# A fifth query normaliser broadcast through DRAM: block 1 of the second linear-attention layer goes from matmul to DMA

## The chip, the cores and the metric

The kernel runs on one core of a Trainium2 chip. The metric is the device time of one execution in microseconds (us), as the median of several runs. The profile is of one more execution; its *span* is 1.7 us shorter than its time (327.5 against 329.18 us before). Engines are named as in the profile: PE (TensorE matmul), PEld (its weight loads), DVE (VectorE), ACT (ScalarE), POOL (GpSimd), SP (SyncE, which issues the DMAs here).

## The reference, cut to what matters

Four layers A, B, A, B on x of 2048 rows by 512 channels, 32 heads of 16 channels, each with a LayerNorm ahead of it and a residual addition behind it. The change lies in the second layer A, a linear attention whose queries pass through two softmaxes:

```python
pq = einsum(q, w_phi)
phi_q = concat([softmax(pq), softmax(-pq)])       # phi_k likewise
kv = einsum("bhsf,bhsd->bhfd", phi_k, v);  z = phi_k.sum(over s)
num = einsum("bhqf,bhfd->bhqd", phi_q, kv)
den = einsum("bhqf,bhf->bhq", phi_q, z) + 1e-6
o = num / den                                     # then @ wo, + x
```

The kernel keeps the plain exponentials `Eq` and multiplies them by one factor per head, sign and position, `rho` = 1/(softmax sum x den). That is the **query normaliser**. `rho` has one row per head, `Eq` has 16 rows per head, so `rho` has to be broadcast 16-fold over partitions.

## The kernel before

The 2048 rows are cut into four blocks of 512. Each stage of a block is a set of small steps; `_ORDER`, a list made beforehand, says in which order all steps of the program are issued, `_CHOICE` says which of the copies and residual additions go to DVE or ACT, and `_SLOTS` which buffer each tile gets. The stage of the query normaliser for layer `L`, block `b`:

```python
_OPT = {"rho_dma": ((0, 2), (0, 3), (1, 2), (1, 3)), ...}   # (layer, block): broadcast by DMA

def s_a3(self, L, b, dma):
    def md(): ...      # PE: 32 matmuls, Eq x z -> denominators in PSUM
    def dr(): ...      # DVE: times 1/softmax sum, both signs added -> Ds
    def ln(): ...      # ACT: Ds -> 1/Ds, as exp(-ln)
    def rho(): ...     # DVE: rS * Ds -> rho, 128 x 2 x 128, bf16

    # by matmul
    def bc(s):         # PE: 16 matmuls with a 0/1 matrix repeat the rows into 4 PSUM tiles
        T["pb", s] = pb = [self.ps() for _ in range(4)]
        for hb in range(NB):
            for t in range(4):
                nc.tensor.matmul(pb[t][:, hb * P:(hb + 1) * P], lhsT=self.indB[32 * t:32 * t + 32, hb, :, :],
                                 rhs=T["rho"][32 * t:32 * t + 32, s, :], start=True, stop=True, tile_position=(32 * t, 0))
    def mulp(s, t, direct):    # DVE: Eq *= PSUM tile (or its SBUF copy by ACT, made by bev)
        ev = self.Eq[L, b][s][:, t, :, :]
        src = T["pb", s][t] if direct else T["bs", s, t]
        nc.vector.tensor_tensor(out=ev, in0=src[:].rearrange("p (a i) -> p a i", a=NB), in1=ev, op=ALU.mult)

    # by DMA; pitch = 16 * 128
    def wr():          # SP: rho to DRAM, 64 KB
        self.RD[L, b] = rd = self.dram.tile([8, 2, pitch], BF16, name="rd%d%d" % (L, b))
        a = rd[0:1, 0, 0:P]
        dst = bass.AP(a.tensor, a.offset, [[P, 16], [2 * pitch, 8], [pitch, 2], [1, P]])
        nc.sync.dma_start(out=dst, in_=T["rho"][:])
    def rdb(s):        # SP: read back, each row to 16 partitions, 512 KB
        rd = self.RD[L, b]
        T["P", s] = pr = self.med([4, NB, P], "Prho")
        a = rd[0:1, s, 0:P]
        src = bass.AP(a.tensor, a.offset, [[2 * pitch, 8], [0, 16], [1, 16 * P]])
        nc.sync.dma_start(out=pr[:].rearrange("p t a i -> p (t a i)"), in_=src)
    def muld(s):       # DVE: one multiplication for half a block
        ev = self.Eq[L, b][s]
        nc.vector.tensor_tensor(out=ev[:], in0=ev[:], in1=T["P", s][:], op=ALU.mult)
    ...                # md, dr, ln, rho; then wr, rdb(0), rdb(1), muld(0), muld(1)
                       # or, for s in 0, 1: bc(s), then 4 times bev(s, t) and mulp(s, t)
```

Behind this stage, block by block: the product `mo` (PE, `Eq` x kv), its eviction `ev` to `oT`, four output matmul groups `mm`, the residual additions `res`, and the LayerNorm of the next layer. (Cuts are marked by "..." or by a comment in place of a body.)

Of the kernel before, what the change touches and what calls it, by code (L numbers as in the profile page):

```python
# [16 lines left out]
P = 128  # L17
NJ = 16
D = 512
H = 32  # L20
# [18 lines left out]
    "rho_dma": ((0, 2), (0, 3), (1, 2), (1, 3)),  # L39
    "tr_dma": (('B0', 1), ('B0', 2), ('B0', 3), ('A1', 0), ('A1', 1), ('A1', 2), ('B1', 1), ('B1', 2), ('B1', 3)),  # L40
    "fold_dma": (),
    "half_k": ((0, 3), (1, 3)),
    "half_ln": (),
    "split": ((1, 2), (1, 3)),
    "v_dram": (),
    "half_mo": (),
    "rho_pad": 0,
# [10 lines left out]
av 8 i i i i i i i i i i i i 0 f 0 g e 2t 0 bs 9 h a d c 0 j k t i i j l 27 o p 3 3 d6 b 1x 1x t 1y o m 2 2 1q  # L58
1z 1x 1x q u t r 1q v x w n s 1r w 1s 4 20 y 21 1x 22 1x 23 1q 1q 1q 1q 1v 1w z 3d 3d 3d 1u 1t 25 3e 3e 3e z 5
3e 3e z z 26 10 18 18 d5 1 z 16 11 4i 15 6 1h 13 3d 3e 3e 25 25 26 18 25 18 12 26 26 28 26 26 26 26 19 12 28  # L60
2a 28 1h 18 14 12 12 1a 28 1c 3e 2g 2g 1f 2h 2h 1h 1h 1b 1i 2b 1b 1e 1d 29 2j 2k 1h 1j 1n 2r 1b 1l 2s 1b 2c 2r
1k 2s 17 2g 2g 2h 2h 1k 1k 2h 2h 2h 2h 2d 1g 2d 2d 2d 2e 2j 1m 35 36 32 2o 2o 33 2s 33 32 33 33 2r 2s 2s 1o 2o
2o 2d 2r 3a 1k 3a 1p 2p 2o 24 24 2s 24 2u 2v 35 37 2u 2u 2u 2s 2i 2w 2j 3a 2s 3a 2l 2z 2j 24 32 32 34 2m 3b 33
3d 3f 3f 2z 2z 2z 33 2f 33 33 2f 2f 2f 3a 3a 2q 2q 2q 30 3a 2n 3a 3a 2z 3e 2q 2x 35 35 b6 3b 3a 2y 31 31 31 31
3c 3c 38 3c 39 3c 3m 3f 3n 3o 3o 3o 24 24 3g 3g 3g 3f 3p 3q 3g 3g 3g 3g 3g 3r 3q 3f 3g 24 3h 3i 3i 5l 5m 5n 3p
3s 3q 3j 3k 3k 3t 3q 3p 3x 5m 3w 3u 3h 3i 3i 3q 3v 3q 3q 3y 3h 3i 3q 3i 3h 3i 3q 5l 5o 5p 5r 5m 5q 7 7 3z 3q
3i 3j 3k 5m 5l 5s 3k 7 7 5m 5m 5m 3h 3i 7g 40 5u 44 41 42 5t 5m 5m 3j 3j 7h 7i 3k 5v 5m 5w 43 7h 45 7j 45 60
3k 3k 3k 46 45 45 5y 5x 5z 61 61 48 47 47 61 49 47 4a 47 4b 62 47 4b 63 3j 4g 94 4c 45 4d 45 4e 4f 3k 45 45 61
64 63 4h 4p 65 95 7j 7j 66 4q 63 96 95 97 97 63 67 7h 63 67 69 7h 6b 4k 4k 4k 4l 4p 4r 4k 4m 4p 4p 4s 4t 7k 7n
6a 68 6c 4o 7m 50 50 4u 4u 4u 4n 4u 7l 4w 97 7o 7p 7p 7q 7s 3l 4x 7r 7r 7p 7t 7p 6o 7u 50 7r 7r 7v 6o 6j 4v 4y  # L70
4j 6o 6q 6o 4j 4z 6k 6p 6r 6j 7r 6e 6l 95 6d 95 7v 6t 6s 6f 6d 7w 6e 7z 7x 98 9b 9a 99 6g 7y 9c 6e 6j 6j 9d 9d
6u 9d 6e 6n 80 6m 9d 6h 6v 6v 9e 9h 9f 6i 9g 9f 6w 6v 6v 6w 6w 9f 9i 9f 87 88 8h 9j 9f 50 82 9j 9l 6w 6x 6x 87
87 6w 81 83 9n 6x 9k 87 8b 89 51 51 51 51 52 52 8c 8c 8e 6u 6u 6u 9m 8j 8a 8d 8c 6v 6y 3l 8f 82 9o 82 85 82 50
51 52 4z 4z 4z 9q 9q 9s 8c 6z 8g 6y 6z 9r 71 70 6y 6y 6z 6z 72 86 a0 a0 a1 73 84 8i 74 75 74 74 50 74 8i 76 8i
77 a2 76 79 53 53 54 55 54 a5 56 53 54 9v 78 76 9q 9q 76 a0 81 53 9v 9w 9p 7a 57 9v 9u a7 76 7a 9t 8j 7c 9y 54
58 59 59 59 9v 59 9x 7d 7e 5a 8j 8j 7b 7f 5c 5b 5d 5b 5b a0 8k 5e 5b 5f 8k 9z a7 5b 5f 5j 8k 8k 8l a3 5i b4 a4
b7 5h b4 b4 b4 8l 5g b5 b5 a7 b5 b5 a7 8k 8l 8j c3 8i c3 b8 c4 c4 c4 c4 a8 8m a8 a8 a8 c3 a9 a9 5k at c1 b5 a6
8m au au c1 c2 b5 c2 aw c2 c2 a8 a9 b5 b5 8n 8o 8n 8p 8m at au at at 8n 8q 8m a7 aa 8n aw 8r 8s au au au 8s 8s
8t au au 8s 8v a6 a6 8u aa 8w aa 8x 8u 8u 8u 8y ab ac ab ad a6 aa b7 8u b9 b7 c3 8y 90 92 c1 91 c1 c2 8z c2 c2
aw ay ab c2 ba ae ab af aw b0 c4 c4 b1 bc ag ag ag ag ah bc aj ak bc c1 c4 c4 bc al ax c3 ai ai ai bd b1 ai am  # L80
93 bf bi bg az bf ai am ar bf bf bg bg aq b7 bg bg bg bg bg bb an ao ag ag ap bi ag ag b1 b1 bc b2 c2 bi bn bi
bl bk as bq br br bq br br bq bq b1 br by by by by bt b3 b3 b3 b3 br be be be br br bz c5 c5 bh bj bn bn bn c5
bu c4 by by by by c6 bo by c6 c6 c5 bt bt bt bn bv c6 c6 c6 bz be bp bp bw bm bp bp c0 c0 by c6 c6 bx c0 c0 c9
c5 ca c6 cb cb cc cb cd ce cd fr fs c7 c8 c7 c8 c8 ft cc ci cf cd cg cd c7 c8 c8 fs fu c8 e2 fu ch cd e3 cd cc
cj ck e4 cd c7 c8 c8 c7 e3 e2 cm cd c8 e6 e7 fu cl cd cd cn cp co e5 e3 hb e3 cr e2 ea e9 cq hc cs e3 cs e8 e3
e3 hd eb ec e3 e3 e3 ed ct cv hc eh cs he ee cs ef cw eg ei cx ei ei cu ei cu cu cu fs cy fs fv ej cu cy d0 cz
ek d2 fw fx fz d3 cs cs fy cs cs g0 g0 g0 el ek em ek en ek d4 d1 dc g1 eo ek g2 g3 g2 dc de eo es g0 g4 dd dh
g2 g5 g2 he hc eq g6 d7 d8 d7 d7 d7 he di dc g2 dc d9 ep er hc et dn hf da db df dh dh dh hi hh hj hg hk hk hk
dj dk dl dm dm g6 g7 g9 dn dn dg ga f0 f0 hl hm hn hm ho hm ev ew f1 hk dn g8 do do hp f2 fa fc hm hq do do dp
ev ex fc gb ev f0 dp ey dn f3 f0 hm fc f4 hq ev ez fc do dp dn dq dq d6 f5 f6 dm dm eu hs gi gj gi fd gs hr fd  # L90
ht fd hu hv fd dq fe fe f5 f5 f8 f5 f9 f7 fb gk fd fe fc gn gn gp gi gi gl gm gd gd gd ge ic gf i7 i7 i9 gg i8
dr dr dt ds dr du hx hy gd dq gu dr dv gn gq gh i7 ff ia gu fb go ff fg fh fb fb eu gv gc gn i2 gr i3 hx hz hx
i7 i2 ib gv i4 hx i1 gc hw i2 i2 i5 gu i0 gu gv gv gw gt ie fg fi if i6 ie id gw if dw dx id gv gw id id ie ie
if if ig dw ff ig if ig fg fj dw e0 dw ff fg fk ie fl fm fl fn gu fl fl fp ih ih ih ih e1 ii ii ii ik ij fq dy
gt gt gt fo fo il io io io io ii im ip iq ip is ir ir ih ii in ip ip iu it ir gx ir gy gx gx gx gz gy h0 dz dz
iv gy h1 h4 gx gy h2 h4 iw iv h5 h5 h6 h7 gy h4 h3 h5 h8 h9 h7 h7 h4 h5 ha h7
# [4 lines left out]
    "0011111111111001110111111010000010010000000000000001011111101100100000110101000110000010000001110111"  # L101
    "1101011110010000110101000000000000001101011000000000100100000000000000000101111100000011011000000000"
    "0000000000001101111010000000100101011111010000011001110111000000000000000111111011101110010100101000"
    "00000000000001111001000000000000000000000000000000000000000000000000000000000001111"
# [5 lines left out]
        "0123456701231231456204632073205712053720457604356704213560421356720415763215063506432506"  # L110
    ),
    "med": (
        "0123456789abcdef5837ae98eeaeae471853bc9e43cbe47199ce3185413cebf94c8f74e3581bc71931bc7f370bf9ac21584e"
        "af9c37214a0b589dec37"
    ),
    "t2": (
        "0123450123450342150132451032451032451032451302153421530421503452014520345123045130425123504321504321"
        "5043215043210451023134"
    ),
    "ps": (  # L120
        "0123456701234750613250746132074365462150743510635127035164051362731405263710452763210743562107423251"
        "0764376215043762435107625407152367423167052341760543210675432170652147053624036542076314257603415203"
        "6415026734107534105234065265346053460562036207346201542015471204712603712035764120356471032516407324"
        "6735012463754021637261350247613025476130746513072463501742635017463015276301562703152760432764327014"
        "6570324650324705613245076"
# [4 lines left out]
class _Fast:  # L130
# [162 lines left out]
    def setup(self):  # L293
        nc, const = self.nc, self.const
        nc.scalar.preload_act_table_set("natural_log_exp_and_others")
        self.WA = const.tile([P, NB, 3 * D], BF16, name="WA")
        self.WoA = const.tile([P, NB, D], BF16, name="WoA")
        self.WB = const.tile([P, NB, 3 * D], BF16, name="WB")
        self.WoB = const.tile([P, NB, D], BF16, name="WoB")
        self.phis = const.tile([P, NB, DH], BF16, name="phis")  # L300
        self.x = [const.tile([P, 4, D], BF16, name="x%d" % b) for b in range(4)]
        with nc.allow_non_contiguous_dma(reason="tiny w_phi load"):
            nc.scalar.dma_start(out=self.phis[:], in_=self.A_w_phi.rearrange("(hb hl) d f -> (hl d) hb f", hb=NB))
        self.wraw = {}
        self.RD = {}
        self.VD = {}
        self.constants()
# [275 lines left out]
    def s_a1(self, L, b):  # L583
# [96 lines left out]
        m = 2 if (L, b) in _OPT["half_k"] else 4  # L680
        for t in range(0, 4, m):
# [89 lines left out]
    def s_a3(self, L, b, dma):  # L771
# [46 lines left out]
        pitch = (16 + _OPT["rho_pad"]) * P  # L818
# [100 lines left out]
    def s_b1(self, L, b):  # L919
# [51 lines left out]
        def vwr():  # L971
            self.VD[L, b] = self.dram.tile([P, NB * KVW], BF16, name="vd%d%d" % (L, b))
            nc.sync.dma_start(out=self.VD[L, b][:], in_=T["V"][:].rearrange("p c t -> p (c t)"))

        def vrep(dl):
# [4 lines left out]
            if (L, b) in _OPT["v_dram"]:  # L980
                a = self.VD[L, b][dl:dl + 1, 2:3]
                src = bass.AP(a.tensor, a.offset, [[2, 4], [4 * NB * KVW, H], [1, VGW]])
# [835 lines left out]
```

## Time and profile before

| | before |
|---|---|
| time, median of 3 runs | 328.98 us (328.91 to 330.25) |
| span of the profiled run | 327.5 us |
| busy: PE, DVE, ACT | 310.3, 302.2, 279.3 us |
| DVE idle in the span | 327.5 - 302.2 = 25.3 us |

The chain of waits of the kernel before (start, duration, what; consecutive instructions of an engine are one line) is followed back only to 219.08 us. From there to 223.7 us it is mostly DVE's multiplications:

```profile
219.08 0.60 DVE Eq L816
...
220.62 3.08 DVE Eq L816 x6
...
223.74 0.57 PE ps L900 x16
```

L816 is `mulp`. This is block 1, the block of the change. SP's timeline shows block 2, which goes by DMA already: its write, and its two reads.

```profile
214.45 0.62 SPq L824 DMA_DIRECT2D rd<-rho  x1
216.66 1.38 SPq L831 DMA_DIRECT2D Prho<-rd  x2
```

Block 1's eight multiplications lie at 218.4 to 223.7 us.

### The profile page before, as it was taken

Reading aid. Unit: us, or ns where it says so; the run is one execution under the profiler, and the core shown is the slowest. Engines: PE = TensorE matmul, PEld = TensorE weight load, DVE = VectorE, ACT = ScalarE, POOL = GpSimd, SP = SyncE. Lnnn points to the kernel's source line nnn. Section 1 sums busy time; section 2 is a strip of 40 time slices with the busy share of each in tenths; the row PEclk is TensorE's granted clock in tenths of the full one; section 3 lists DMA queues with packets and bytes.
Section 4 is the critical chain, followed back from the end, with each engine's and each line's share of the span. In section 5 each row is a group of like instructions: output and inputs, shape, how many; then the busy total and the mean of one; then the engine's idle time right before and its main releaser. Section 6 shows DMA issues by size and latency. Waiting matters only on the chain. (4 is left out here: it accounts for less than half of the span.)

```text
span 327.5 us, 8033 instructions
## 1 busy us (share of the span) xinstructions
PE 310.3 (95%) x3176; PEld 149.5 (46%) x3203; DVE 302.2 (92%) x439; ACT 279.3 (85%) x634; POOL 25.3 (8%) x50
## 2 busy tenths in 40 slices
PE   7999999999999999999999999979999999999873
PEld 3655456445444444443444455644544454433221
DVE  7998995998998999899999999699999999999993
ACT  5999988998888999989999999798999996676550
POOL 4000000000021003000000000000000208400000
PEclk9999999999999999999999999999999999999999
DMA  7980000004556899998750300023436977679952
GB/s 197 380 197 3 0 2 4 2 20 120 105 148 135 152 164 133 139 121 154 137 135 1 67 3 2 4 59 90 128 58 125 179 146 134 150 139 158 166 176 92
DMA packets 37388, 35.41 MB, mean 108 GB/s; under 512 B 23008, under 2 KB 32224, under 8 KB 37344
## 3 DMA queue, kind: packets, MB, share of 16 engines
q1 hardware_dynamic: 36816, 34.81, 53.6%
q8 instruction: 27, 0.44, 0.6%
q14 instruction: 17, 0.14, 0.2%
q10 hardware_dynamic: 528, 0.02, 0.1%
HBM read 10.50 MB, written 2.36 MB: 39 GB/s over the span
## 5 line engine op out<-in xcount | busy, mean ns | idle before, releaser
L927 PE MATMUL ps<-xnT,WB 128*128 128x512 bf16 x384 | 87.6, 380 | 0.5 <-DMA xnT<-xn 0.5
L1081 DVE TENSOR_TENSOR pav<-PT,Vg 128x4096 bf16<-128x4096 bf16 (+1 forms) x34 | 72.0, 2162 | 1.5 <-DMA Vg<-V 1.0
L1019 DVE TENSOR_TENSOR prod<-QT,K 128x4096 bf16<-128x4096 bf16 x32 | 72.5, 2291 | 0.3 <-ACT QT L192 0.2
L927 PEld LDWEIGHTS <-WB 128*128 128x128 bf16 x384 | 42.3, 114 | 43.3 <-issue 5.8
L520 PEld LDWEIGHTS <-oT 128*128 128x128 bf16 x256 | 23.8, 97 | 34.5 <-ACT oT L192 5.7
L192 ACT CAST oT<-ps 128x512 bf16<-128x512 f32 (+1 forms) x60 | 32.1, 587 | 8.4 <-PE ps L1090 7.1
L706 ACT ACTIVATE Eq<-ps 128x512 bf16<-128x512 f32 x64 | 34.0, 615 | 0.7 <-PE ps L698 0.6
L520 PE MATMUL ps<-WoB,oT 128*128 128x512 bf16 x122 | 32.1, 380 | 2.4 <-ACT oT L192 2.0
L599 ACT ACTIVATE Ek<-ps 128x512 bf16<-128x512 f32 x64 | 33.6, 622 | 0.4 <-PE ps L593 0.2
L698 PE MATMUL ps<-xnT,WA 128*128 128x512 bf16 x128 | 30.7, 380 | 0.6 <-DVE Eq L816 0.6
L540 ACT ACTIVATE sqd<-x 128x512 bf16<-128x512 bf16 x48 | 30.1, 643 | 1.0 <-DVE x L533 0.8
L605 PE MATMUL ps<-WA,xnT 128*128 128x512 bf16 x120 | 30.0, 380 | 0.5 <-issue 0.2
L593 PE MATMUL ps<-WA,xnT 128*128 128x512 bf16 x124 | 29.7, 380 | 0.6 <-DMA xnT<-xn 0.2
L520 PE MATMUL ps<-WoA,oT 128*128 128x512 bf16 x120 | 29.2, 380 | 0.4
L533 DVE SCALAR_TENSOR_TENSOR x<-ps,x 128x512 bf16<-128x512 f32 x38 | 25.4, 686 | 1.9 <-PE ps L520 1.7
L192 ACT CAST V<-ps 128x512 bf16<-128x512 f32 x31 | 17.5, 595 | 4.4 <-PE ps L927 4.3
L192 ACT CAST K<-ps 128x512 bf16<-128x512 f32 x31 | 17.8, 585 | 3.7 <-PE ps L927 3.3
L530 ACT ACTIVATE x<-ps 128x512 bf16<-128x512 f32 x26 | 15.1, 598 | 6.4 <-PE ps L523 6.3
L192 ACT CAST QT<-ps 128x512 bf16<-128x512 f32 x29 | 17.1, 592 | 2.5 <-PE ps L927 2.5
L651 DVE TENSOR_TENSOR Ek<-Ek,rk 128x4096 bf16<-128x4096 bf16 (+1 forms) x10 | 18.6, 1858 | 0.5 <-ACT rk L646 0.5
L593 PEld LDWEIGHTS <-xnT 128*128 128x128 bf16 x128 | 12.1, 97 | 15.4 <-DMA xnT<-xn 0.7
L446 ACT ACTIVATE xn<-x,nmr,rstd 128x512 bf16<-128x512 bf16 x23 | 18.2, 822 | 1.0 <-DVE nmr L435 0.8
(129 smaller groups left out, 433.3 us busy)
## 6 DMA issues: line engine op xcount, KB each, us to landing
Vg<-V SPq DMA_DIRECT2D x128, 131.5 KB, 4.4
Prho<-rd SPq DMA_DIRECT2D x8, 512.0 KB
x<-in_A_x_dram SPq DMA_DIRECT2D x3, 512.0 KB
WB<-in_B_wqkv_dram SPq DMA_DIRECT2D x3, 512.0 KB, 11.6
wraw<-in_A_wqkv_dram SPq DMA_DIRECT2D x4, 256.0 KB, 4.5
out_dram<-x SPq DMA_DIRECT2D x4, 256.0 KB, 2.2
out_dram<-x SPq DMA_DIRECT2D x8, 128.0 KB, 2.2
x<-in_A_x_dram SPq DMA_DIRECT2D x4, 128.0 KB
```

What stands on the lines that cost most here:

```text
L192: self.nc.scalar.copy(out=out, in_=in_)
L520: nc.tensor.matmul(y[:], lhsT=oT[:, c, t * P:(t + 1) * P], rhs=Wo()[:, c, :], start=(c == 0), stop=(c == NB - 1 and not onpe))
L533: nc.vector.scalar_tensor_tensor(out=xb[:, t, :], in0=T[t][:], scalar=1.0, in1=xb[:, t, :], op0=ALU.mult, op1=ALU.add, **kw)
L540: nc.scalar.activation(out=sqd[:], in_=xb[:, t, :], func=ACT.Square, accum_out=T["ss"][:, t:t + 1])
L593: nc.tensor.matmul(pk[:], lhsT=xnT[:, t, k, :], rhs=self.WA[:, k, D:2 * D], start=(k == 0), stop=(k == NB - 1))
L599: nc.scalar.activation(out=T["E"][:, t, s, :], in_=T["k", t][:], func=ACT.Exp, scale=1.0 - 2.0 * s)
L605: nc.tensor.matmul(pv[:], lhsT=xnT[:, t, k, :], rhs=self.WA[:, k, 2 * D:3 * D], start=(k == 0), stop=(k == NB - 1))
L698: nc.tensor.matmul(pq[:], lhsT=self.WA[:, k, hb * P:(hb + 1) * P], rhs=xnT[:, :, k, :], start=(k == 0), stop=(k == NB - 1))
L706: nc.scalar.activation(out=self.Eq[L, b][s][:, :, hb, :], in_=T[hb][:].rearrange("p (t i) -> p t i", t=4), func=ACT.Exp, scale=1.0 - 2.0 * s)
L927: nc.tensor.matmul(pp[:], lhsT=self.WB[:, k, i * D + c:(i + 1) * D:NB], rhs=xnT[:, :, k, :], start=(k == 0), stop=(k == NB - 1))
L1019: nc.vector.tensor_tensor(out=pr[:], in0=QT[:, c:c + 1, :].to_broadcast([P, NW, TB]), in1=win, op=ALU.mult)
L1081: nc.vector.tensor_tensor(out=pv, in0=PT[:, :, lo:lo + n].unsqueeze(1).to_broadcast([P, NB, 2, n]), in1=vw, op=ALU.mult)
```

## The change

The intent is to apply to block 1 what blocks 2 and 3 have: 32 small matmuls and eight multiplications, mostly from PSUM, against one write, two reads and two multiplications from SBUF. The core of the diff:

```diff
-    "rho_dma": ((0, 2), (0, 3), (1, 2), (1, 3)),
+    "rho_dma": ((0, 2), (0, 3), (1, 1), (1, 2), (1, 3)),
...
-    "half_k": ((0, 3), (1, 3)),
+    "half_k": {(0, 3): 1, (1, 3): 1},        # the same halves, written another way
-    "v_dram": (),                            # switches that were off
-    "rho_pad": 0,
...
 _ORDER = """ ... """                         # all of it replaced
 _CHOICE = ( ... )                            # all of it replaced
 _SLOTS = { ... }                             # all of it replaced
```

In the new order block 1's query stage comes first, then blocks 2 and 0; the denominators of all three are made before anything is multiplied.

## The prediction

> **What bounds the kernel now.** I read the busy times of the page first, then the busy time by stretch, then the groups of instructions, then the chain that ended last.
>
> ```profile
> span 327.5 us, 8033 instructions
> PE 310.3 (95%) x3176; PEld 149.5 (46%) x3203; DVE 302.2 (92%) x439; ACT 279.3 (85%) x634; POOL 25.3 (8%) x50
> PE 26%; DVE 3%; ACT 2%; issue 1%; DVEq 0%
> ```
>
> Three engines are nearly full. The chain of waits is PE for most of its length (26% of the span against 3% for DVE), so no engine stands waiting for one partner. Outside the two ends, this is a work-bound kernel: what moves its time is work taken off PE or DVE, or a gap closed on them. The stretches around the change, in busy time of each engine, granted clock, DMA share and GB/s, are these:
>
> ```profile
> 208.00:213.00 5.00, 4.59 (x138) 2.74 (x131) 2.53 (x9) 3.35 (x8) 0.00 (x0) 1.00 0.03 7
> 213.00:217.00 4.00, 3.04 (x68) 1.49 (x67) 3.97 (x9) 3.92 (x11) 0.00 (x0) 1.00 0.09 16
> 217.00:219.00 2.00, 1.84 (x68) 1.14 (x68) 2.00 (x6) 1.97 (x6) 0.00 (x0) 1.00 0.24 84
> 219.00:221.00 2.00, 1.36 (x49) 0.89 (x48) 1.77 (x6) 2.00 (x6) 0.00 (x0) 1.00 0.49 121
> 221.00:223.00 2.00, 1.95 (x14) 0.89 (x10) 2.00 (x4) 1.89 (x6) 0.00 (x0) 1.00 0.49 131
> 223.00:225.00 2.00, 1.95 (x39) 0.70 (x38) 1.69 (x5) 1.30 (x4) 0.00 (x0) 1.00 0.53 131
> 225.00:227.00 2.00, 1.95 (x10) 0.93 (x10) 2.00 (x7) 2.00 (x6) 0.00 (x0) 1.00 0.45 102
> 227.00:229.00 2.00, 2.00 (x11) 0.90 (x10) 1.90 (x4) 1.97 (x9) 0.00 (x0) 1.00 0.01 4
> ```
>
> The first engine column is PE, the third DVE, the fourth ACT. The second layer A normalises its queries between 208 and 223 us. From 208 to 221 PE is idle 0.41 + 0.96 + 0.16 + 0.64 = 2.17 us while DVE is full from 213 on: here DVE, with the PSUM multiplications, holds PE back. Later, by coarser stretches, DVE is busy 19.91 of 20 us (260 to 280), 20.00 of 20 (280 to 300) and 15.00 of 15 (300 to 315), while PE falls to 18.75 and 12.24 in the last two. So the last 35 us end on DVE, and DVE work removed anywhere after 208 can count, if it lets that dense phase begin earlier. The clock is 1.00 here, so no throttle is involved.
>
> [...] the multiplication of a 128x512 piece costs 682 ns from PSUM and 416 ns from SBUF, and 128x2048 in one piece 1224 ns.
>
> ```profile
> L816 DVE TENSOR_TENSOR Eq<-ps,Eq 128x512 bf16<-128x512 f32 x25 | 16.1, 682 | 0.1
> L835 DVE TENSOR_TENSOR Eq<-Eq,Prho 128x2048 bf16<-128x2048 bf16 x8 | 9.7, 1224 | 0.0
> L808 PE MATMUL ps<-rho,indB 32*128 32x128 bf16 x128 | 4.3, 217 | 0.6 <-ACT oT L192 0.5
> L816 DVE TENSOR_TENSOR Eq<-bs,Eq 128x512 bf16<-128x512 bf16 x7 | 2.9, 416 | 0.0
> L846 ACT CAST bs<-ps 128x512 bf16<-128x512 f32 x7 | 4.1, 589 | 0.0
> ```
>
> [...] The four writes of rho to DRAM (64 KB) land after 2.1 to 3.9 us, median 3.0[...]. [...] I use 0.216 us for a 128x512 matmul, from the chain (36 of them in 7.77 us).
>
> **The change, part by part.** Only block 1 of the second layer A goes over to DMA. The matmul broadcast of it goes: 32 matmuls of 32x128, 4.3/128 = 0.034 us each, so PE -1.07 us. Its eight multiplications go; in the choice string of before six read PSUM and two a copy by ACT: 6 x 0.682 + 2 x 0.416 = 4.92 us of DVE. Two multiplications of 128x2048 come: 2 x 1.224 = 2.45. DVE -2.48 us. ACT loses two copies, 2 x 0.589 = -1.18 us. SP gains one write and two reads of 512 KB.
>
> The diff also replaces the order of all steps, the buffer slots and the assignment of work to DVE or ACT. I counted the assignments in the two strings. Residual additions: five more move from DVE to PE and ACT: DVE -5 x (0.686 + 0.083), one without the accumulator, = -3.76; PE +5 x 0.216 = +1.08; ACT about +3.81 (5 x 0.598 + 4 x 0.204). Six more 128x512 evictions go to DVE: +6 x 0.686 = +4.11, ACT -6 x 0.59 = -3.5. Two more LayerNorm applications on DVE: +2 x 0.408 = +0.82, ACT -2 x 0.82 = -1.64. Two more broadcast pieces of other blocks pass through ACT: DVE -2 x 0.266 = -0.53, ACT +1.18. The transposed copies net to DVE +0.42, ACT -0.5. The removed switches (a DRAM path for V, a pitch) were off, and the new form of the half option gives the same halves, so none of them costs anything.
>
> Sums: PE -1.07 + 1.08 = 0.0; DVE -2.48 - 3.76 + 4.11 + 0.82 - 0.53 + 0.42 = -1.42; ACT -1.18 + 3.81 - 3.5 - 1.64 + 1.18 - 0.5 = -1.8 us. So the gain on PE is spent at once on residual additions that relieve DVE. Counting only steps after 208 us, DVE loses some 0.8 and PE 0.2 us. The four residuals of block 3 (4 x 0.77 = 3.1 us of DVE, at 247 to 253) move to PE just where the dense DVE phase begins, and four more evictions of block 0 (2.7 us) come shortly before.
>
> What of this reaches the end: up to 0.8 us of work after 208, perhaps 0.3 from before it, and some of PE's 2.17 us of gaps, since the eight PSUM buffers and the DVE time of one broadcast no longer stand between PE and its next matmuls. I choose a third of these gaps, 0.7 us: 0.8 + 0.3 + 0.7 = 1.8, so 329.0 - 1.8 = 327.2 us.
>
> **The rivals.** First, the DMA as the new wait. In before, block 2 goes this way: rho is ready at 214.4, the reads are issued from 216.7, and the DMA runs at 84 to 131 GB/s until about 226.5; its first multiplication starts at 226.75. That is about 12 us for both halves, an estimate from the windows. In the new order block 1 is handled first and block 0 keeps the matmuls. On DVE, between rho of block 1 and its first multiplication stand the two other blocks' denominators (2.3 us with rho), a small product (0.4), block 0's eight multiplications (5 x 0.682 + 3 x 0.416 = 4.7) and two evictions (1.4), so about 8.8 us; then 1.2 us and three residuals (2.3), about 12.3 us to the second. This is just in time, with block 2's write in front of the second read on SP. A late read would stall DVE in order, 0 to 2 us, and give 327 to 330 us. Against more: DVE's own gaps add slack, and the same path in before shows no DVE wait for Prho.
>
> Second, PE as the bound with its work unchanged: if PE and not DVE sets the length from 223 to 290 us (PE is idle under 0.3 us from 223 to 231), the DVE relief is worth nothing and the time stays at about 329. The long chain of PE speaks for it, the full DVE from 260 on against.
>
> Third, the new order as such. It touches every stage, the loads at the start too (one x piece and the V weights later). A better packing could close part of the 6.6 us that DVE idles from 50 to 100 us, giving 324 to 325; a worse one could cost as much.
>
> **Range and chances.** The counted work moves by at most 1.4 us on a full engine, the rest is packing, which I hold to about 2.5 us either way: 324.6 to 329.6. Faster by over 2% would need 6.6 us, more than the change removes from any engine; slower by 2% would need a long stall that an order fitted to this change should not have. Chances 0.03 faster, 0.95 the same, 0.02 slower.
>
> **What would show it.** Right: 96 instead of 128 broadcast matmuls; ten multiplications of 128x2048 at 1.22 us; DVE busy near 300.8 and PE near 310.3 us; no wait of DVE for Prho above 1 us; the stretch after the query normalisation shorter by about 1.5 us; ends alike. Wrong: DVE idle before the new multiplications, released by DMA; PE gaps in the 30 us after the key-value product as large as before; or a difference that is already there before 200 us, which would belong to the new order and not to the broadcast.

## The result, and the profile after

| | before | after |
|---|---|---|
| time, median (4 runs each, same rounds) | 328.95 us (328.6 to 330.25) | 332.97 us (332.25 to 334.34) |
| ratio | | 1.012, 95% interval 1.0077 to 1.0163 |
| span | 327.5 us | 330.4 us |
| busy PE, DVE, ACT | 310.3, 302.2, 279.3 | 310.8, 301.0, 279.4 |
| DVE idle in the span | 25.3 us | 330.4 - 301.0 = 29.4 us |

A ratio here is the mean time of one kernel's fast runs over that of the kernel before in the same rounds on the same chip, so it is not quite the ratio of the medians quoted. The kernel became 1.2% slower, and its time lies above the predicted range of 324.6 to 329.6 us.

Below are the head of the page, the engines' busy times and the shares of the chain that ended last. (These shares can't be set beside the 26% of PE in the prediction: the chain of the kernel before covers only its last third, this one the whole span.)

```profile
span 330.4 us, 7970 instructions
PE 310.8 (94%) x3148; PEld 150.6 (46%) x3176; DVE 301.0 (91%) x433; ACT 279.4 (85%) x634; POOL 35.4 (11%) x50
PE 67%; DVE 8%; ACT 8%; DMA 6%; SPq 3%; POOL 3%; issue 2%; DVEq 0%; ACTq 0%; POOLq 0%
```

DVE's work fell by 1.2 us and DVE's idle time rose by 4.1: the sum is the 2.9 us of the span. The groups show that the operations are those expected: ten large multiplications, 96 broadcast matmuls, 24 multiplications of pieces in place of 32 (17 from PSUM, below, and 7 from SBUF).

```profile
L832 DVE TENSOR_TENSOR Eq<-Eq,Prho 128x2048 bf16<-128x2048 bf16 x10 | 12.1, 1220 | 0.2 <-DMA Prho<-rd 0.2
L813 DVE TENSOR_TENSOR Eq<-ps,Eq 128x512 bf16<-128x512 f32 x17 | 10.8, 682 | 0.5 <-PE ps L805 0.5
L805 PE MATMUL ps<-rho,indB 32*128 32x128 bf16 x96 | 2.9, 216 | 2.2 <-DVE rho L798 1.4 <-DVE Eq L813 0.4 <-ACT Eq L703 0.3
```

The first line also says that DVE waited for the new transfers 0.2 us in the whole program. The loss is not a wait for DMA by name. Where it sits is told by busy time in stretches. First the stretch from 200 to 230 us of the kernel before (window, length, PE, PEld, DVE, ACT, POOL with instruction counts, clock, DMA share, GB/s):

```profile
200.00:230.00 30.00, 27.63 (x561) 14.68 (x578) 26.06 (x53) 26.66 (x67) 0.00 (x0) 1.00 0.18 45
```

and the same of the kernel after:

```profile
200.00:230.00 30.00, 25.35 (x521) 13.39 (x522) 21.86 (x47) 23.00 (x57) 0.15 (x1) 0.94 0.29 76
```

DVE's idle time at 200 to 230 us went from 30 - 26.06 = 3.9 to 30 - 21.86 = 8.1 us: +4.2, as much as the whole rise. (By the same view, ahead of 200 us it fell by 1.7, at 230 to 260 it rose by 0.9, after that by 0.7. POOL is busy 10 us longer, since its 18 small copies took 29.9 us and not 19.9, but DVE waits only 0.6 us for one of them. DVE work that was done before 200 us leaves a hole after it, so not all of the 4.2 us need be loss; e2 below has 2.0 us of it and loses nothing.) So the query stage of the second layer A is where to look; e2 and e3 below test it. The chain of waits there, now of the kernel after:

```profile
209.45 0.97 ACT Eq L703 x2
210.43 0.30 ACT Ds L793
...
210.75 0.31 ACT Ds L794
...
211.68 1.06 ACT Eq L703 x2
212.75 0.30 ACT Ds L793
...
213.07 0.32 ACT Ds L794
...
213.41 0.44 DVE rho L798
...
213.89 0.43 PE ps L805 x16
214.31 1.29 DVE Eq L813 x2
```

From 208.0 to 213.4 us the chain stays on ACT: the small operations `ln` of one denominator after another, each between DVE's `dr` and `rho` (2.0 us in all), and between them exponentials of the queries `Eq` (2.0) and softmax sums (1.0). ACT is busy 4.87 of 5 us at 208 to 213, where it was busy 3.35 before. The waits name the denominators too (waits of DVE at 200 to 232 us: total, times, longest). In the kernel before:

```profile
DVE rho L801 <- ACT Ds L797: 0.8, 1, 0.8
...
DVE oT L190 <- PE ps L900: 0.3, 1, 0.3
```

In the kernel after:

```profile
DVE rho L798 <- ACT Ds L794: 2.5, 3, 0.9
...
DVE oT L188 <- PE ps L897: 2.0, 2, 1.4
```

In the kernel before, the second and third denominators lie between multiplications of block 0, and DVE waits for `ln` only once. And the timeline of DVE in the kernel after shows how long the broadcast of block 1 really had: `rho` at 208.77, the multiplications at 221.00 and 224.13.

```profile
208.77 0.43 DVE L798 TENSOR_TENSOR rho<-rS,Ds 128x256 bf16<-128x256 f32 x1 [0.81 <-ACT Ds L794]
...
221.00 1.22 DVE L832 TENSOR_TENSOR Eq<-Eq,Prho 128x2048 bf16<-128x2048 bf16 x1
...
224.13 1.22 DVE L832 TENSOR_TENSOR Eq<-Eq,Prho 128x2048 bf16<-128x2048 bf16 x1
```

Between this `rho` and the first of them DVE had two more denominators, the eight multiplications of block 0, a small product and two evictions, 7.87 us of work in 11.80; ACT was busy 10.47 us of it (order of columns as above):

```profile
209.20:221.00 11.80, 8.87 (x177) 4.17 (x175) 7.87 (x17) 10.47 (x24) 0.00 (x0) 0.86 0.41 106
```

One more thing is new in this stage: the granted clock of PE falls to one half for some 3.4 us, from about 215.7 to 219.2 us (0.87 at 215 to 216, 0.50 in each us to 219, 0.92 at 219 to 220). (A second drop lowers it to 0.89 at 300 to 315 us, where DVE is busy 15.00 of 15 us, before as after.)

```profile
213.00:214.00 1.00, 0.11 (x9) 0.13 (x13) 0.42 (x1) 0.97 (x4) 0.00 (x0) 1.00 0.65 197
214.00:215.00 1.00, 0.55 (x19) 0.26 (x13) 0.70 (x2) 1.00 (x3) 0.00 (x0) 1.00 0.55 131
...
216.00:217.00 1.00, 1.00 (x4) 0.27 (x2) 1.00 (x4) 1.00 (x3) 0.00 (x0) 0.50 0.52 117
```

A matmul of the `Eq` projections (128x512) took 607 ns at 215.8 to 219.1 us, against 381 ns at 205 to 213. In the stretch ahead of the drop, 212.3 to 215.7 us, PE was busy 1.79 of 3.4 us; in the kernel before it was busy 3.06 us of the same stretch, and the clock stayed at 1.00. What makes the clock fall isn't shown. Three causes could explain the loss: the latency of the broadcast (through the order that was made to hide it), the new order as such, and the clock.

### The profile page after: what moved, and what is told of

It reads as the page before. It is cut to its first block, busy times and chain, and to the rows that moved or that the text cites.

```text
span 330.4 us, 7970 instructions
## 1 busy us (share of the span) xinstructions
PE 310.8 (94%) x3148; PEld 150.6 (46%) x3176; DVE 301.0 (91%) x433; ACT 279.4 (85%) x634; POOL 35.4 (11%) x50
## 4 chain that ended last, share of the span: by engine, by line
PE 67%; DVE 8%; ACT 8%; DMA 6%; SPq 3%; POOL 3%; issue 2%; DVEq 0%; ACTq 0%; POOLq 0%
PE ps L924 15%; PE ps L517 13%; PE ps L590 8%; PE ps L602 8%; PE ps L695 7%; DVE prod L1005 3%; DMA Vg<-V 3%; PE ps L1076 3%; POOL vh L966 3%; SPq L976 3%; PE ps L1012 2%; PE ps L665 2%; DVE pav L1067 2%; DMA xnT<-xn 2%; PE ps L457 2%
## 5 line engine op out<-in xcount | busy, mean ns | idle before, releaser
L190 ACT CAST oT<-ps 128x512 bf16<-128x512 f32 (+1 forms) x57 | 30.2, 582 | 6.8 <-PE ps L1076 5.7
L517 PE MATMUL ps<-WoB,oT 128*128 128x512 bf16 x122 | 33.6, 392 | 1.3 <-ACT oT L190 0.6
L695 PE MATMUL ps<-xnT,WA 128*128 128x512 bf16 x128 | 32.1, 387 | 0.4 <-DVE Eq L813 0.2
L602 PE MATMUL ps<-WA,xnT 128*128 128x512 bf16 x121 | 29.9, 379 | 0.5 <-issue 0.2
L527 ACT ACTIVATE x<-ps 128x512 bf16<-128x512 f32 x31 | 18.2, 594 | 8.9 <-PE ps L520 8.7
L966 POOL COPY vh<-V 128x64 bf16<-128x64 bf16 x6 | 17.2, 2871 | 78.6 <-ACT V L190 78.6
L530 DVE SCALAR_TENSOR_TENSOR x<-ps,x 128x512 bf16<-128x512 f32 x33 | 21.9, 686 | 1.2 <-PE ps L517 0.9
L1076 PE MATMUL ps<-pav,indAV 128*32 128x512 bf16 (+1 forms) x272 | 17.1, 369 | 3.0 <-DVE pav L1067 2.9
L602 PEld LDWEIGHTS <-xnT 128*128 128x128 bf16 x128 | 12.2, 98 | 14.1 <-issue 0.4
L590 PEld LDWEIGHTS <-xnT 128*128 128x128 bf16 x128 | 11.9, 98 | 14.5 <-issue 1.3
```

What stands on the lines that cost most here:

```text
L190: self.nc.scalar.copy(out=out, in_=in_)
L517: nc.tensor.matmul(y[:], lhsT=oT[:, c, t * P:(t + 1) * P], rhs=Wo()[:, c, :], start=(c == 0), stop=(c == NB - 1 and not onpe))
L590: nc.tensor.matmul(pk[:], lhsT=xnT[:, t, k, :], rhs=self.WA[:, k, D:2 * D], start=(k == 0), stop=(k == NB - 1))
L602: nc.tensor.matmul(pv[:], lhsT=xnT[:, t, k, :], rhs=self.WA[:, k, 2 * D:3 * D], start=(k == 0), stop=(k == NB - 1))
L695: nc.tensor.matmul(pq[:], lhsT=self.WA[:, k, hb * P:(hb + 1) * P], rhs=xnT[:, :, k, :], start=(k == 0), stop=(k == NB - 1))
L966: nc.gpsimd.tensor_copy(out=self.vh[L, b][:], in_=T["V"][:, :, TB:KVW])
```

## The experiments

The theories. **Latency:** block 1's eight multiplications were useful filler while block 2's broadcast was on its way; by DMA, block 1 has a latency of its own and no filler. **Order:** the new order of all steps is worse, broadcast or not. **Clock:** PE at half speed stretches the stage. Two baselines recur: "the old order" is that of the kernel before, "the new order" that of the kernel after. In kernels e1, e7, e9, e12 and e13 only the steps of the query stage are moved (in e12 also block 0's output matmuls and residual additions). DVE idle below is 30 us less DVE's busy time at 200 to 230 us of the profiled run; it includes the stage but also where the stage happens to lie. How much that is worth shows in e2: level with before, and yet 2.0 us more idle.

| run | median us | ratio | 95% | DVE idle |
|---|---|---|---|---|
| before (329.6 to 330.2 in these rounds) | | 1 | | 3.9 |
| after | 332.97 | 1.012 | 1.0077 to 1.0163 | 8.1 |
| e1: old order, block 1 by DMA | 340.41 | 1.0328 | 1.0289 to 1.0366 | 10.9 |
| e2: new order up to the z product, then old, by matmul | 330.08 | 0.9996 | 0.9981 to 1.001 | 5.9 |
| e3: old order up to the z product, then new, by DMA | 335.08 | 1.014 | 1.0121 to 1.016 | 7.4 |
| e4: after, with extra matmuls | 333.11 | 1.0089 | 1.0064 to 1.0115 | 9.0 |
| e5: new order, block 1 by matmul | 343.94 | 1.0411 | 1.0385 to 1.0436 | 13.9 |
| e6: after, block 0's denominator second | 334.32 | 1.0125 | 1.0106 to 1.0145 | 9.6 |
| e7: e1 with reads of 16 rows | 332.66 | 1.0088 | 1.0069 to 1.0106 | 8.7 |
| e8: e6 with reads of 16 rows | 333.93 | 1.0147 | 1.01 to 1.0194 | 8.8 |
| e9: e1, block 1 without latency | 330.88 | 1.0026 | 0.9982 to 1.0069 | 7.4 |
| e10: after with reads of 16 rows | 332.7 | 1.0114 | 1.0078 to 1.0151 | 8.2 |
| e11: before with reads of 16 rows | 328.92 | 0.9989 | 0.9959 to 1.0018 | 3.9 |
| e12: e7 with other steps between | 332.26 | 1.0084 | 1.0056 to 1.0113 | 8.3 |
| e13: e1, blocks 1 and 2 without latency | 329.43 | 0.999 | 0.9973 to 1.0007 | 5.5 |
| e14: before, block 2 without latency | 329.05 | 0.9979 | 0.9963 to 0.9995 | 4.1 |

### e1 and e5: the broadcast and the order, each alone

e1 takes the kernel before and moves block 1 alone to DMA. Its denominator changes place with block 2's, so that its write comes first:

```diff
-    "rho_dma": ((0, 2), (0, 3), (1, 2), (1, 3)),
+    "rho_dma": ((0, 2), (0, 3), (1, 1), (1, 2), (1, 3)),
 order: md, dr, ln, rho of block 1 <-> those of block 2; wr, rdb(0), rdb(1) of block 1 where block 2's were,
        block 2's wr right behind its rho, its reads after; muld(0), muld(1) of block 1 at the places of mulp(1,2), mulp(1,3)
```

> The kernel before, its order and assignments kept, with the broadcast of block 1 of the second layer A by DMA alone: block 1 takes the place of block 2 in the line of denominators, its two multiplications of 128x2048 stand where its last two multiplications by PSUM stood. Order theory (the loss of the change lies in the new order of the query normalisation, where three denominators in series stand before any multiplication): 327.5 to 330.5 us, DVE idle between 200 and 230 us near the 3.9 us of before, perhaps 1 to 2 us of DVE wait for the transfer set against 2.5 us less DVE work. Broadcast theory (the transfer by DMA costs the time itself): 331.5 us or more. Clock theory (PE's clock, halved for 3.4 us after a gap of PE, is the loss): 328 to 330 with a clock of 0.998, 331.5 or more if the clock falls.

Measured: 10 us slower than before. DVE waits 9.0 us for the reads (6.0 for block 1's, 3.0 for block 2's), and block 2's small write, issued at 218.42 behind block 1's two large reads (216.98), lands only after almost 10 us (waits of DVE in e1, and its DMA issues with KB and us to landing, which this trace gives for one write only; in the kernel before, block 2's write was issued at 214.45 and its reads could start at 216.66, 2.2 us later):

```profile
DVE Eq L833 <- DMA Prho<-rd: 9.0, 4, 3.3
```

```profile
rd<-rho SPq DMA_DIRECT2D x5, 64.0 KB, 9.7
```

1 MB of reads at the 133 GB/s of this trace (shown under e7) takes 8 us, an estimate, which fits a write that lands only after them; that it waited for them is our reading. So the broadcast of block 1, put in where the matmuls were, costs far more than it saves. (The clock falls too: 0.95 at 200 to 230 us, 0.82 at 230 to 240.)

e5 is the opposite: the new order with block 1 by matmul again, `bc`, `bev` and `mulp` at the places of `muld`.

```diff
-    "rho_dma": ((0, 2), (0, 3), (1, 1), (1, 2), (1, 3)),
+    "rho_dma": ((0, 2), (0, 3), (1, 2), (1, 3)),
 order: muld(h) of block 1 -> bc(h), then bev(h, t), mulp(h, t) for t = 0 to 3; its wr and rdb dropped;
        block 1's rho in another buffer, since it is kept longer
```

> The changed kernel with its order, but block 1 broadcast by matmul again: 32 matmuls and eight multiplications stand where the two multiplications of 128x2048 stood. Order theory: the idle time of the query normalisation stays and 2.5 us of DVE and 1.1 of PE come on top, so 334 to 337 us. Broadcast theory: 329 to 331.

Measured: 14 us slower than before, outside both expectations. The matmuls stand where `muld` stood, behind block 0's product, and the clock was 0.83 at 200 to 230 us, so part of the 14 us may be the price of that place; no run separates it. In these placements neither half of the change can be had by itself. What the two runs say together is that the new order *repairs* most of e1's loss (10 us to 4), and that the loss can't be split into a part of the order and a part of the broadcast.

### e2 and e3: which part of the order

Both cut the two orders at the same step, just behind the second half of the z product, and join them; e2 has the new one first and block 1 by matmul, e3 the old one first and block 1 by DMA.

```diff
 order: steps of one kernel up to and with z(1) of the second layer A, then the other kernel's remaining steps in its own order
```

> The order of the changed kernel up to the second key-value product, then the order of before, block 1 by matmul. Order theory: 326.5 to 329.5 us, since the loss lies behind this cut and the changed kernel had 1.7 us less DVE idle time before 200 us. If the loss came from the first 200 us: 331.5 or more. Broadcast and clock theory: 327 to 330, clock at 0.998.

> The order of before up to the second key-value product, then that of the changed kernel with the broadcast of block 1 by DMA. Order, broadcast and clock theory: 332 to 336 us, DVE idle 7 us or more between 200 and 230 us. If the loss came from the first 200 us: 328 to 330.

Measured: e2 is level with before (0.9996), e3 is 1.4% slower. The two thirds of the program ahead of the z product don't matter; the loss lies behind it. And e3, whose head is that of the kernel before, has 7.4 us of DVE idle time against 3.9, with a full clock (window 200 to 230 us of e3):

```profile
200.00:230.00 30.00, 24.18 (x534) 12.76 (x527) 22.61 (x44) 22.81 (x53) 0.00 (x0) 1.00 0.24 62
```

### e4: the clock

e4 keeps PE busy in the kernel after by four matmuls of 128x512 with an unused result ahead of each broadcast of block 0:

```diff
             T["pb", s] = pb = [self.ps() for _ in range(4)]
+            if (L, b) == (1, 0):
+                for _ in range(4):
+                    nc.tensor.matmul(pb[0][:], lhsT=self.ident[:], rhs=self.WoA[:, 0, :], start=True, stop=True)
```

> The changed kernel with 8 more matmuls of 128x512 that nobody reads, four ahead of each of the two matmul broadcasts of block 0 in the second layer A, where PE stands idle for 0.9 and 0.4 us before its clock is halved (about 215.8 to 219.2 us). Clock theory: the clock stays at 1.00 there and the time falls to 329 to 330 us. Order theory: the clock stays but the time falls by 0.5 to 1.5 us only, to 331.5 to 332.5. Broadcast theory: no change, 333.

Measured: the clock was 1.00 at 210 to 220 us, but the drop came later instead (0.83 at 220 to 230), and the time is that of the kernel after, not the 329 to 330 us of the clock theory. Taken alone this is inconclusive. The profiled runs of e3, and of e10 further down, have the loss without the drop, so **the clock isn't what the loss needs**; it may still add something within the intervals, which are 0.2 to 0.4% wide to each side. The single runs say the same: one of the four of the kernel after had a mean clock of 0.995, as the kernel before has it (0.995 to 1.000), and took 332.74 us; the other three, at 0.981 to 0.987, took 332.25 to 334.34.

### e6 and e8: another order for the stage, a failed repair

e6 takes the kernel after and reorders its query stage by hand: block 0's denominator second, block 2's between the multiplications, a second buffer for `Ds`.

```diff
-            T["Ds"] = self.sm([P], "Ds", F32, 1)
+            T["Ds"] = self.t2([P], "Ds", F32) if (L, b) == (1, 0) else self.sm([P], "Ds", F32, 1)
 order: block 1's and block 0's denominators, then block 0's multiplications with block 2's dr, ln, rho between them
```

> The changed kernel with one stretch reordered: the last query projection of block 0 comes before that of block 2, the denominator of block 0 comes second instead of third (with a second buffer for it), and that of block 2 goes between block 0's multiplications. Block 1 stays by DMA. Order theory: DVE idle between 200 and 230 us falls from 8.1 to 5 or 6 us, no PE gap near 213, clock at 1.00 there, 329.5 to 331.5 us. Broadcast theory: 332.5 to 334.

Measured: a miss, 1.0125, no better than the kernel after. The first multiplication did come 1.5 us earlier (212.82 against 214.30), but block 0's product began at about 219 us in both. The buffers of my order were at fault in part: PE stood 1.9 us for a PSUM tile that DVE still had to read. e8 is e6 with reads of 16 rows (below), and moved by less than the intervals.

> The reordered stretch of the sixth experiment with the 16-row writes and reads of the seventh. Order theory: DVE of the changed kernel did not wait for Prho, so a faster read alone gives within 0.7 us of the sixth experiment. If the transfer is hidden cause of other waits (the write of block 2 behind the reads of block 1): 1 us or more faster than it.

Nothing about the cause follows from these two, except that an earlier start of block 0's multiplications alone doesn't help.

### e7, e10, e11: a shorter transfer

The reads of 512 KB ran at a DMA share of one half (0.49 to 0.53 at 219 to 225 us of the kernel before). On the DRAM side their outer dimension has 8 rows; that the share hangs on these rows was a guess, which e7 tests. These three kernels write `rho` twice and read with 16 outer rows:

```diff
-    rd = self.dram.tile([8, 2, pitch], BF16, ...)      # one write of 64 KB
+    rd = self.dram.tile([16, 2, pitch], BF16, ...)     # each row twice: four writes of 32 KB
...
-    src = bass.AP(a.tensor, a.offset, [[2 * pitch, 8], [0, 16], [1, 16 * P]])
+    src = bass.AP(a.tensor, a.offset, [[2 * pitch, 16], [0, 8], [1, 16 * P]])
```

> The first experiment (order of before, block 1 by DMA) with rho written twice to DRAM (four writes of 32 KB), so that each read of 512 KB has 16 rows instead of 8 as its outer dimension. If the reads ran on half of the DMA engines because of the 8 rows (the DMA share of the trace stood at 0.50 at 131 GB/s): share near 1.0, twice the rate, DVE's wait for Prho falls from 9.0 to some 4 us, 334 to 337 us instead of 340. If another limit sets the rate: 340 us, share still at 0.5.

> The changed kernel, but rho is written to DRAM twice (four writes of 32 KB) so that the reads have 16 outer rows instead of 8; in e7 that took the reads from a DMA share of 0.50 to 0.85. Theory (the changed kernel's order has already moved its denominators to the front, so VectorE waits for no transfer there and the loss is the idle time of that order): 332 to 334, as the changed kernel. Rival (the length of the transfer still costs in the changed kernel): 329 to 330.5.

> The kernel before, block 1 still by matmul, with the same 16 rows for the four blocks that it broadcasts by DMA already. Theory (before has filler for those transfers; VectorE waits under 0.3 us for Prho there): 328.3 to 329.8, as before. Rival (the transfers cost the kernel before too, through queueing): under 328.

With 16 rows the DMA share was 0.90 in place of 0.50, and the rate 209 in place of 133 GB/s. (Whether half of the DMA engines stood idle with 8 rows isn't shown: the share is a mean over all of them.) The same window of e1 and of e7 (the last two columns are the DMA share and GB/s):

```profile
221.00:223.00 2.00, 1.62 (x8) 0.69 (x8) 0.00 (x0) 1.69 (x5) 0.00 (x0) 1.00 0.50 133
```

```profile
221.00:223.00 2.00, 1.88 (x24) 0.63 (x22) 1.23 (x1) 1.33 (x4) 0.00 (x0) 1.00 0.90 209
```

With this e1's order falls from 340.4 to 332.7 us (below the 334 to 337 expected), and DVE's wait for Prho from 9.0 to 3.6 us. Apart from the small writes only the length of the transfers differs, so **about 8 of e1's 10 us hang on how long the transfers take**. The kernel before doesn't gain (e11, 0.9989): its transfers were covered. The kernel after doesn't gain either (e10, 1.0114). That its order has already paid for the longer transfers, in idle time, is the reading that fits; it is argued and not shown, for the reason given below. The stage of e10 has the same hole, at a clock of 1.00 throughout (e10):

```profile
200.00:230.00 30.00, 23.89 (x525) 13.09 (x526) 21.77 (x47) 22.89 (x57) 0.15 (x1) 1.00 0.32 81
```

The blemish of e10: the four writes hold the buffer of `rho` longer, and DVE waits 1.7 us for that, a wait that the kernel after doesn't have. So e10 can't say what fast reads alone would give there.

e12 tried to fill the rest of e7's gap, by putting block 0's last two output matmuls and its residual additions ahead of block 1's second multiplication.

```diff
 order: muld(0), muld(1), mo of block 1; res, mm(2), mm(3) of block 0
     -> mm(2), mm(3), res(0), muld(0), res(1), rho and wr of block 3, res(2), res(3), muld(1), mo of block 1
```

> e7_before_dma16 with the fill put back: block 0's last two output matmuls and its four residual additions are moved ahead of block 1's second DMA multiplication and of its second product, so that VectorE and TensorE have something to do while block 1's reads come in. Theory (the loss is latency without filler): the wait for Prho falls from 3.6 us to under 2 us, TensorE's idle 2.5 us before block 1's product shrinks below 1.5 us, and the time is 329.5 to 331.5, below e7's 332.7. Rival (the loss of e7 is elsewhere): 332.5 or more.

Measured: a miss, 1.0084 against e7's 1.0088. The wait for Prho went from 3.6 to 2.9 us, but block 1's product came later in turn, and DVE was idle 15 - 9.98 = 5.0 us at 215 to 230 us against 5.5. That too little other work of the right kind was at hand is our reading.

### e9, e13, e14: no latency at all

To take the latency away without taking a needed wait away, the reads take old data: rows that the first layer's blocks left in DRAM long before. The values are wrong. (The comparison with the reference isn't sharp enough to tell these normalisers apart, and nothing rests on it.) e9 does this for block 1 in e1's order, the reads issued at 190 us instead of 217:

```diff
-            rd = self.RD[L, b]
+            rd = self.RD[(0, 3) if (L, b) == (1, 1) else (L, b)]
...
-            add(st, "SP", wr)
+            if (L, b) != (1, 1):
+                add(st, "SP", wr)
 order: rdb(0), rdb(1) of block 1 about 40 steps ahead of the z product
```

> Wrong result on purpose: e1_before_dma (the old order, block 1 by DMA), but the two reads of block 1 take rows that block 3 of the first layer had left in DRAM long ago, and are issued some 20 us earlier, ahead of the z product; block 1's 64 KB write is dropped. The work on every engine stays that of e1, only the latency of the broadcast is gone. Theory (the work saved is real, what was lost is the wait for the transfer and what queues behind it): VectorE's wait for Prho falls from 9.0 us to under 2 us, and the time to 326.5 to 330.0, so 10 us or more below e1 and level with or below the kernel before. Rival 1 (without the eight multiplications there is nothing to fill block 2's transfer and block 0's chain, so the idle time only moves): VectorE idle at 200 to 230 us stays above 7 us and the time is 331 to 335. Rival 2 (the order of e1 was broken in another way): 335 or more.

Measured: ratio 1.0026, level with before, so 3% or some 10 us better than e1. (The profiled run, 332.49 us, was the slowest of the four; the other three lie at 328.9 to 331.3.) This is the main proof for the old order: with the same work on every engine, the latency of one broadcast and what queues behind it make the difference; the two are not told apart. The expectation of 326.5 to 330.0 us was missed by a little. The time is not below before, and DVE's idle time of 7.4 us is what the rival expectation had named (above 7). DVE has a new wait, for **block 2's** reads, which the kernel before covers with block 1's multiplications (waits of DVE in e9):

```profile
DVE Eq L833 <- DMA Prho<-rd: 2.5, 1, 2.5
```

e13 therefore takes away the latency of both, and e14 is its control, the kernel before with block 2's taken away. The edit is that of e9 with blocks 1 and 2 (e13) or block 2 alone (e14) in the conditions, block 2 reading what the first layer's block 2 left.

> Values not its own, on purpose: e9 with the reads of block 2 taken early from old rows in DRAM as well (both small writes dropped). Theory (latency without filler is all of the loss): no wait for Prho of blocks 1 and 2, VectorE busy above 13 of 15 us at 215 to 230 us, and the time 327 to 328.8, under its control e14 by about the 1.2 us of saved VectorE work. Rival (the chain from block 0's and block 1's products through eviction, output matmul and residual addition holds the stage once its filler has gone): VectorE still idle for over 3.5 us there and the time 329.5 to 331, over its control.

> Values not its own, on purpose: the kernel before (block 1 by matmul) with block 2's two reads taken early from old rows in DRAM and its small write dropped. The control for e13. Both theories: VectorE does not wait for Prho in before, so 328 to 329.8, ratio 0.997 to 1.001.

Measured, at five rounds: e13 0.999 (0.9973 to 1.0007), e14 0.9979 (0.9963 to 0.9995). With no latency left, the DMA form in this order is level with the matmul form; it isn't faster. Neither expectation of e13 came true as a whole. If the 1.2 us of saved DVE work that it named had come through, e13 would stand at 0.9979 - 1.2/329.6 = 0.994, outside its interval. The same stretch of e13 and of e14 shows where the saving goes:

```profile
215.00:230.00 15.00, 12.76 (x208) 5.75 (x193) 12.89 (x28) 13.78 (x38) 0.00 (x0) 1.00 0.11 27
```

```profile
215.00:230.00 15.00, 13.18 (x244) 6.59 (x237) 14.33 (x32) 14.07 (x38) 0.00 (x0) 1.00 0.05 9
```

DVE has 14.33 - 12.89 = 1.44 us less to do, and is idle 1.44 us longer. Its waits in e13 are for ACT's sums of block 3 (1.2 us) and for PE's product of block 1 (0.7 us), against 0.2 and 0.3 us in those places of e14: DVE arrives earlier and waits for the others. One of these waits belongs to the order, though (timeline of DVE in e13):

```profile
220.62 0.42 DVE L788 TENSOR_TENSOR s<-ps,rS 128x256 f32<-128x256 f32 x1 [1.16 <-ACT rS L719]
```

This is block 3's `dr`. Block 1's two multiplications are issued behind it, at 221.29, although their reads had been issued by 204.9 us. Nobody moved one of them (1.22 us) into the hole of 1.16 us. So e13 shows that the saving is lost in this order, not that every order must lose it.

No run with right values beats the kernel before; e11 is level with it.

## Why the prediction was wrong

**The work terms of DVE and PE held.** Predicted: PE 0, DVE -1.42, ACT -1.8 us. Measured: PE +0.5, DVE -1.2, ACT +0.1. Counts and durations of the new operations were as worked out (ten multiplications of 1.22 us, 96 matmuls). PE's sum missed by 0.5 us and ACT's by 1.9; neither explains a rise of 4. (ACT's groups in the trace do add up to some 4 us less, 319.5 to 315.5, but its busy time is 279.3 and 279.4: groups overlap in time, so sums of durations are not busy time.)

**The step that failed is "what of this reaches the end".** It credited 0.8 us of the work after 208 us, 0.3 us from before, and a third of PE's gaps at 208 to 221 us, together -1.8 us. The time rose by 4.0 us instead. In place of the 1.8 us of gain, DVE's saved work ended as idle time, and the order that makes room for the transfer added more of it. Two errors are in that step:

- *It treated the stage as bound by DVE's work.* The text read "here DVE, with the PSUM multiplications, holds PE back". e13 against e14 is that claim tested without any latency: in that order the saved DVE work turned one for one into idle time. Nor do its own lines have DVE "full from 213 on": it is busy 1.77 of 2 us at 219 to 221, and 0.41 of the 2.17 us of PE's gaps lie at 208 to 213, where DVE is half idle (2.53 of 5). The lines that the prediction itself shows could have warned: from 213 to 221 us ACT is busy 3.92 + 1.97 + 2.00 = 7.89 of 8 us, as full as DVE (7.74). That ACT was the partner that set the pace there is a reading of these lines and of e13's waits; no run changed ACT's work alone.
- *It missed that the removed work was the cover for another transfer.* The multiplications of block 1 filled the time of block 2's broadcast. Taken away, they leave a second transfer and no filler. e1 shows the full price when the order stays (+10 us, 9.0 us of it in DVE's wait for Prho), e7 and e9 that the price goes with the latency (to 1.0088, to 1.0026), and e9's new wait of 2.5 us for block 2 that the filler role was real.

**The first rival came nearest, by another path.** It named the DMA as the new wait, put the latency at about 12 us for both halves and saw that the transfer would be "just in time"; it gave 327 to 330 us. The late read that it feared didn't come (multiplications at 221.00 and 224.13, no wait). What failed is that it added up DVE's work as if DVE would do it without a gap: 8.8 us from `rho` to the first multiplication, 12.3 to the second. It took 12.2 and 15.4 us, with 3.9 us of idle time in the first stretch (11.80 - 7.87). The kernel after draws three denominators to the front, whose `ln` steps stand behind one another on ACT, and DVE runs dry. That this order was made so in order to hide the latency is our reading; no run takes the latency out of the new order. The sign to look for, "no wait of DVE for Prho above 1 us", came true and said nothing: DVE's longer waits stand under other names, `ln` and block 0's product. The sign that did report it was the one in the same list, "PE gaps in the 30 us after the key-value product as large as before": PE's idle time at 200 to 230 us went from 30 - 27.63 = 2.4 to 30 - 25.35 = 4.7 us.

**The second rival**, that DVE relief is worth nothing, describes e13 (though not with PE as the bound: PE is idle 15 - 12.76 = 2.2 us there). **The third**, the new order as such, is not a cause of its own as far as the runs go: its head is neutral (e2), its tail carries the loss (e3), and without the DMA broadcast, in the placement of e5, it is worse still.

**PSUM against SBUF.** The 682 and 416 ns that the prediction gives for a piece of 128x512 are a factor of 1.64; four pieces from PSUM (4 x 682 ns) against one operation of 1224 ns are a factor of 2.2. Its estimates use the durations, so nothing hangs on either factor.

**What stays open.** How much the half clock added in the kernel after (e4 only moved it; e3 and e10 have the loss without it). How much of e1's loss is block 1's own latency and how much is block 2's write issued behind its reads; no run took another queue for either. Whether ACT set the pace of the new stage; no run moved its exponentials. And whether a better order of this stage exists for five DMA blocks: e6, e8 and e12 were three tries by hand, none came to the kernel before, and the hole in e13 was not filled.

## What to carry to other kernels

Before work is taken out of a stage, ask what runs under it: operations that look like cost may be the cover of a transfer, and a broadcast through DRAM (a write, two reads; some 12 us in the kernel before for 64 KB out and 1 MB in, an estimate from block 2's write at 214.45 us and a DMA share of 0.01 at 227 to 229) has to find its own cover in work that doesn't depend on it (in e1 DVE waited 6.0 us for block 1's reads). A schedule that avoids the wait by issuing everything earlier may only rename it, as here; compare the time and the idle time of the stage, not the wait for the transfer. And a test with old data in place of the new (no dependence, same work) separates what a transfer costs in latency from what it saves in work, before anyone tunes an order for it.
